# A Fourier-mixing and max-out feed-forward kernel: batch 0's loads in twelve transfers, and late work moved on GpSimd

## The chip, the cores and the metric

The kernel runs on one NeuronCore of a Trainium2 chip. The metric is the device time of one execution in microseconds (us); the time of a kernel is the median of its runs. Engines are named as in the profile: PE (TensorE, with PEld for its weight loads), DVE (VectorE), ACT (ScalarE), POOL (GpSimd) and SP (SyncE, which here only issues transfers).

## The reference

The input is x, 8 batches of 3072 rows by 256 columns, and four weight matrices. What is computed:

```
X = fft(fft(x, axis=1), axis=2).real          # 8 x 3072 x 256, then 24576 x 256
h = max(X @ w1, X @ w2, X @ w3)               # 24576 x 768
out = h @ w_out                               # 24576 x 256
```

## The kernel before

**Tiling.** The transform over the 3072 rows is split as 24 x 128. In a first stage ("s", lines 492 and 494; seven pieces per batch) PE multiplies batch b's rows with small 24-point matrices. The rows lie on 96 partitions (24 row groups times 4 column groups), once in natural order and once reversed. In a second stage ("k", lines 518 and 520; six pieces per batch) PE multiplies the result z with the table `tab`. This table has 13 row blocks of 384 values: sines, cosines, and negated sines. The transform over the 256 columns never runs on data: it is folded into the weights at the start (`prep_first`, `prep_second`), with the matrix `md`.

**Units.** The feed-forward part then runs per batch in 18 units (3 blocks of 512 tokens times 6 slices of the hidden width). A unit has four "plus" matmuls (538, 539), ACT's Relu (552), DVE's maximum (553), two "minus" matmuls (546), and about nine matmuls of the output layer (563). Of each 128 output rows (a slot, 12 in a batch), DVE makes `other` (590), POOL adds it to `even` (593), DVE adds that to PE's sum (613), and POOL and SP store the two halves (616, 626).

**Order.** The order on each engine is the order in which the program issues instructions. The dictionary `plan` (784 to 808) lists which extra work is issued at the end of which unit. `at(b, unit, fn)` adds to it. A unit number of 18 or more falls into the next batch. The engines run in order, so an instruction that waits holds all that stands behind it on its engine.

**Batch 0.** Its rows 112 to 127 come on the SP and ACT queues as fp32 (`xs_a`, 202). Rows 0 to 111 come on POOL's software queue, which casts them to bf16: three groups of 32 rows and one of 16, each group in four transfers (209 to 211). Then POOL issues w1 in two halves (219). SP issues raw w2 and w3 in four transfers (222); the first two wait for the second transfer of the last group of rows. SP has one queue, so batch 1's rows (409) stand behind these. ACT and DVE copy each group that has landed into a natural (`lay_rows`, 365) and a reversed (`turn_rows`, by way of `reverse`, 136) layout, each with the columns split between them. Among these copies DVE makes table angles (`tab_angles`, 270 and 274: two instructions for three row blocks), ACT the sines (`tab_sines`, 281 to 285), and DVE the argument `vm` of `md`. PE meanwhile runs 31 matmuls on table data (709) that nothing reads.

**POOL at the start.** After its transfers POOL waits for the last of DVE's copies (411), does some small constants and `rows_m` (412 to 237), the second halves of the differences w2 - w1 and w3 - w1 (`differences`, 186), and issues w_out (418). Then come batch 1's casts, per chunk of 32 rows one natural (151) and one reversed (154). `tab_minus` (289) negates the sines of table rows 7 to 9 at unit 1 and of rows 10 to 12 at unit 3, between the casts. PE's k pieces 3 and 4 read these.

**Later batches.** Rows are fetched by SP in four chunks (`fetch`, 771) into a ring of four buffers and cast by POOL. For batch 2 the 16 casts (4 chunks in 4 parts) are issued two per unit in units 14 to 21, counted from batch 0's first unit. For batches 3 to 7 they are one per unit from unit 6 of the batch two before.

Of the kernel before, what the change touches and what calls it, by code (L numbers as in the profile page):

```python
# [33 lines left out]
def kernel(  # L34
# [50 lines left out]
    two_row = consts.tile([128, 128], BF16, tag="two_row")  # L85
    half_pi = consts.tile([128, 64], FP32, tag="half_pi")
    w_late = consts.tile([128, 6 * 128], FP32, tag="w_late")
    twice = consts.tile([128, 256], FP32, tag="twice")
    sgn = consts.tile([128, 1], FP32, tag="sgn")
    dif = consts.tile([128, 1], FP32, tag="dif")  # L90
# [110 lines left out]
    rows_a = xs_a[:, 0:17 * 64].rearrange("p (bb dl) -> p bb dl", dl=64)  # L201
# [4 lines left out]
    iota(pidx, [[0, 1]], cm=1)  # L206
    j128 = gen.tile([128, 128], FP32, tag="j128")
    iota(j128, [[1, 128]])
    for r0 in (0, 32, 64):
        load_rows(nc.gpsimd, x0v[:, r0:r0 + 32, :], 0, r0, r0 + 32)  # L210
    last_part = load_rows(nc.gpsimd, x0v[:, 96:112, :], 0, 96, 112)

    def load_w(eng, wdst, wsrc, jh):
        return eng.dma_start(  # L214
# [5 lines left out]
    for jh in range(2):  # L220
        for wsrc, wdst in zip((moe_w2, moe_w3), raw_w):
            ld = load_w(nc.sync, wdst, wsrc, jh)
            if jh == 0:
                tc.add_manual_dep(ld.ins, last_part[1].ins.name, AFTER, reason="x first")

    rows_f = gen.tile([128, 12 * B], FP32, tag="rows_f")
    late = gen.tile([128, 1], FP32, tag="late")
# [23 lines left out]
    pi13 = gen.tile([128, 13], FP32, tag="pi13")  # L251
# [3 lines left out]
    step = gen.tile([128, 128], FP32, tag="step")  # L255
# [8 lines left out]
    def rows_of(r0, r1):  # L264
        return (w_late if r0 >= 7 else w)[:, (r0 % 7) * 128:(r0 % 7 + r1 - r0) * 128]

    def tab_angles(r0, r1):
        wr = rows_of(r0, r1)
        n = r1 - r0
        nc.vector.tensor_tensor(  # L270
            out=wr.rearrange("p (r j) -> p r j", j=128),
            in0=pi13[:, r0:r1].unsqueeze(2).to_broadcast([128, n, 128]),
            in1=step.unsqueeze(1).to_broadcast([128, n, 128]), op=ALU.subtract)
        nc.vector.scalar_tensor_tensor(out=wr, in0=wr, scalar=0.5, in1=wr,
                                       op0=ALU.is_gt, op1=ALU.subtract)

    def tab_sines(r0, r1, parts=(0, 1, 2)):
        wf = rows_of(r0, r1)
# [79 lines left out]
    def turn_rows(copy, r0, n, d0, d1):  # L358
        reverse(copy, xr0, x0_first[:, r0 * 64:(r0 + n) * 64], r0, n, d0, d1)
# [13 lines left out]
    lay_rows(on_act, xs_a, 112, 16)  # L373
    reverse(on_dve, xr0, xs_a, 112, 17)
    on_dve(out=xr0[:, 32, 17:18], in_=xs_a[:, 0:1])
    turn_rows(on_act, 0, 31, 32, 65)
    tab_angles(7, 10)
    tab_angles(10, 13)
    vm = gen.tile([128, 256], FP32, tag="vm")
    qm = gen.tile([128, 256], FP32, tag="qm")  # L380
    nc.vector.tensor_scalar(out=vm[:, 0:128], in0=dvec, scalar1=pidx, scalar2=64.0,
                            op0=ALU.mult, op1=ALU.add)
    lay_rows(on_act, bf_rows(0, 32), 0, 32)
    tab_sines(7, 10, (0, 1))
    turn_rows(on_dve, 31, 32, 32, 65)
    lay_rows(on_dve, bf_rows(32, 32), 32, 32)
    nc.vector.tensor_scalar(out=vm[:, 128:256], in0=dvec, scalar1=pidx, scalar2=None,
                            op0=ALU.mult)
    nc.vector.tensor_scalar(out=vm[:, 128:129], in0=pidx, scalar1=128.0, scalar2=64.0,
# [1 line left out]
    nc.vector.tensor_scalar(out=qm, in0=vm, scalar1=256.0 * ROUND, scalar2=None, op0=ALU.add)  # L391
    nc.vector.scalar_tensor_tensor(out=vm, in0=qm, scalar=-256.0 * ROUND, in1=vm,
                                   op0=ALU.add, op1=ALU.subtract)

    nc.scalar.activation(out=md[0], in_=vm, func=AX.Sin, scale=float(-2.0 * math.pi / 256.0))
    for (copy, a, b, c, d) in ((on_act, 54, 65, 20, 33), (on_dve, 32, 54, 0, 20)):
        turn_rows(copy, 63, 32, a, b)
        lay_rows(copy, bf_rows(64, 32), 64, 32, c, d)
    for (copy, a, b, c, d) in ((on_act, 58, 64, 22, 33), (on_dve, 32, 58, 0, 22)):
        turn_rows(copy, 95, 17, a, b)  # L400
        if copy is on_act:
            turn_rows(copy, 95, 16, 64, 65)
        laid = lay_rows(copy, bf_rows(96, 16), 96, 16, c, d)
    nc.vector.tensor_scalar(out=sgn, in0=pidx, scalar1=0.0, scalar2=None, op0=ALU.is_equal)
    nc.vector.tensor_scalar(out=sgn, in0=sgn, scalar1=2.0, scalar2=-1.0,
                            op0=ALU.mult, op1=ALU.add)
# [1 line left out]
    for ch in range(4):  # L408
# [5 lines left out]
    nc.gpsimd.memset(gw[:, 512:513], 0.0)  # L414
    nc.gpsimd.memset(gw[0:1, 512:513], 1.0)
    store_rows()
    differences(nc.gpsimd, 1)
    nc.gpsimd.dma_start(out=wout_bf.rearrange("p (jc c) -> p jc c", jc=NJC),
                        in_=moe_w_out.rearrange("(jc p) c -> p jc c", jc=NJC))

    def wide(t, cs):
        return t.rearrange("p (fc j) -> p fc j", fc=2)[:, :, cs]
# [348 lines left out]
    def fetch(b, ch):  # L771
        raw[b, ch] = load_chunk(b, ch)
# [11 lines left out]
    for (u, fn) in ((0, prep_some), (0, prep_some), (0, lambda: tab_sines(7, 10, (2,))),  # L784
                    (1, prep_some), (1, prep_some), (1, prep_some),
                    (2, lambda: m.k(2)), (2, prep_some), (2, lambda: tab_sines(10, 13, (0,))),
                    (3, prep_some), (3, lambda: tab_sines(10, 13, (1, 2))),
                    (4, lambda: m.k(3)), (4, prep_some), (5, prep_some), (5, l2_first),
                    (6, lambda: m.k(4)), (7, lambda: m.k(5)), (7, m.end),
                    (0, lambda: turn_chunk(1, 0)), (1, lambda: tab_minus(7, 10, nc.gpsimd)),  # L790
                    (2, lambda: turn_chunk(1, 1)), (3, lambda: tab_minus(10, 13, nc.gpsimd)),
                    (5, lambda: turn_chunk(1, 2)),
                    (7, lambda: turn_last(0)), (8, lambda: turn_last(1)),
                    (8, lambda: lay_last(0)), (9, lambda: lay_last(1)), (20, signed)):
        at(0, u, fn)
    for ch in range(4):
        at(0, (6, 7, 9, 11)[ch], lambda ch=ch: fetch(2, ch))
    for b in range(B - 1):
        for i, whats in enumerate(ahead):
            for what in whats:  # L800
                at(b, begin[b] + i if b else first_ahead[i], lambda b=b, what=what: piece(b + 1, what))
        if b + 2 < B:
            for ch in range(4):
                for part in range(4):
                    at(b, 6 + 4 * ch + part if b else 14 + 2 * ch + part // 2,
                       lambda b=b, ch=ch, part=part: turn_chunk(b + 2, ch, part))
                if b + 3 < B:
# [80 lines left out]
```

## Time and profile before

| what | value |
|---|---|
| median of three runs | 416.93 us (414.61 to 417.04) |
| the profiled execution | 416.61 us |
| its span, first to last instruction | 414.8 us |
| PE busy | 394.1 us, 95% of the span |
| POOL busy | 318.2 us, 77% |
| DVE busy | 309.2 us, 75% |
| ACT busy | 266.9 us, 64% |
| PE clock granted | 1.00 |
| DMA packets | 131175, 52.70 MB |

The profile is that of one execution. Its lines give a start, a duration, the engine, the line of the kernel, the operation, the tiles (out<-in) and, in brackets, how long the engine stood idle before and what ended that. The view by stage gives busy times and instruction counts of each engine between two times. A matmul's end is modelled, so short overlaps on PE mean nothing. The chain that ended last is followed back from the last instruction, at each step to what released it.

### The profile page before, as it was taken

The page shows a single profiled execution, that of the slowest core. Times are in us where ns is not written, and L with a number is a line of the kernel's source. Part 1 is how long each engine was busy: PE and PEld are TensorE (multiplying, and loading weights), DVE is VectorE, ACT ScalarE, POOL GpSimd, SP SyncE. Part 2 cuts the span into 40 slices and gives each one's busy share as a digit, 9 for nine tenths or more (in the row PEclk, how much of TensorE's full clock was granted, in tenths as well). Part 3 has the DMA queues.
Part 4 walks back from the last instruction along what each step waited for, and adds up shares of the span by engine and source line. Part 5 has one row for each costly group of instructions (what it writes and reads, how often), then busy time and mean ns, then how long its engine had stood idle before and what let it go on. Part 6 is the DMA issues. An engine that isn't in the chain of part 4 may idle for free.

```text
span 414.8 us, 9054 instructions
## 1 busy us (share of the span) xinstructions
PE 394.1 (95%) x3018; PEld 268.4 (65%) x3072; DVE 309.2 (75%) x559; ACT 266.9 (64%) x491; POOL 318.2 (77%) x429
## 2 busy tenths in 40 slices
PE   0988899989999999999999999999999999999996
PEld 0455667756676677667666666666676677766665
DVE  8887676776777777787668767687678777778884
ACT  7877667656765666756775666666676666655550
POOL 9846977999998888888878788888878844545651
PEclk9999999999999999999999999999999999999999
DMA  9998896574317852398216843287412222111314
GB/s 113 141 217 161 173 224 164 154 192 108 123 67 186 195 140 74 96 216 168 97 64 162 205 107 110 88 206 171 133 52 76 66 66 76 66 65 46 110 64 141
DMA packets 131175, 52.70 MB, mean 127 GB/s; under 512 B 113073, under 2 KB 128184, under 8 KB 131128
## 3 DMA queue, kind: packets, MB, share of 16 engines
q1 hardware_dynamic: 106496, 37.50, 36.6%
q0 software_dynamic: 23696, 14.29, 15.5%
q8 instruction: 24, 0.39, 0.4%
q10 hardware_dynamic: 936, 0.33, 0.3%
q14 instruction: 23, 0.19, 0.2%
HBM read 29.02 MB, written 25.17 MB: 131 GB/s over the span
## 4 chain that ended last, share of the span: by engine, by line
PE 86%; SPq 5%; POOL 4%; DMA 2%; issue 1%; DVE 0%; POOLq 0%
PE po L563 29%; PE pse L538 15%; PE pse L546 14%; PE pse L539 12%; SPq L103 4%; POOL x L103 3%; PE po L587 3%; PE ps L518 2%; PE ps L494 2%; PE ps L520 2%; PE ps L492 2%; PE pl L576 2%; DMA xs<-in_x_dram 1%; DMA x<-in_x_dram 1%; SPq L214 1%
## 5 line engine op out<-in xcount | busy, mean ns | idle before, releaser
L552 ACT ACTIVATE stmp<-pse 128x512 bf16<-128x512 f32 x288 | 171.2, 600 | 45.1 <-PE pse L539 26.7
L553 DVE TENSOR_TENSOR hp<-pse,stmp 128x512 bf16<-128x512 f32 x144 | 99.5, 691 | 89.4 <-ACT stmp L552 59.1
L616 POOL DMA_INDIRECT out_dram<-ot,rows_m x92 | 102.5, 1114 | 53.8 <-DVE ot L613 40.8
L538 PE MATMUL pse<-t,gE 128*128 128x512 bf16 x288 | 109.3, 379 | 2.1
L553 DVE TENSOR_TENSOR hm<-pse,stmp 128x512 bf16<-128x512 f32 x144 | 99.1, 689 | 3.7 <-ACT stmp L552 3.5
L539 PE MATMUL pse<-t,gO 128*128 128x512 bf16 x249 | 94.3, 379 | 0.0
L563 PE MATMUL po<-wout_bf,hp 128*128 128x256 bf16 x576 | 85.9, 273 | 0.0
L563 PE MATMUL po<-wout_bf,hm 128*128 128x256 bf16 x570 | 85.3, 273 | 0.1
L593 POOL TENSOR_TENSOR even<-even,other 128x256 f32<-128x256 f32 x92 | 66.5, 723 | 22.7 <-DVE other L590 20.4
L546 PE MATMUL pse<-t,gD 128*128 128x512 bf16 x273 | 82.4, 379 | 0.7
L563 PEld LDWEIGHTS <-hp 128*128 128x128 bf16 x576 | 56.2, 98 | 18.0 <-issue 2.8
L563 PEld LDWEIGHTS <-hm 128*128 128x128 bf16 x576 | 56.3, 98 | 16.6
L613 DVE TENSOR_TENSOR ot<-po,even 128x512 f32<-128x512 f32 x92 | 62.7, 682 | 0.7 <-POOL even L593 0.7
L151 POOL CAST x<-xs 96x544 bf16<-96x544 f32 (+2 forms) x51 | 58.7, 1155 | 4.6 <-DMA xs<-in_x_dram 4.6
L154 POOL CAST x<-xs 96x544 bf16<-96x544 f32 (+5 forms) x57 | 60.5, 1070 | 0.0
L522 ACT CAST t<-ps 128x512 bf16<-128x512 f32 x48 | 27.9, 585 | 36.5 <-PE ps L520 35.3
L546 PEld LDWEIGHTS <-gD 128*128 128x128 bf16 x288 | 27.9, 98 | 32.2
L499 ACT CAST z_all<-ps 128x480 bf16<-128x480 f32 x46 | 25.4, 559 | 35.2 <-PE ps L494 34.2
L590 DVE SCALAR_TENSOR_TENSOR other<-twice,po 128x256 f32<-128x256 f32 x92 | 43.8, 476 | 0.1
L539 PEld LDWEIGHTS <-gO 128*128 128x128 bf16 x288 | 28.1, 98 | 20.0 <-issue 1.8
L538 PEld LDWEIGHTS <-gE 128*128 128x128 bf16 x288 | 28.1, 98 | 19.9 <-issue 0.7
L579 ACT COPY even<-pl 128x512 f32<-128x512 f32 x46 | 27.0, 587 | 9.6 <-PE pl L576 9.2
(168 smaller groups left out, 382.9 us busy)
## 6 DMA issues: line engine op xcount, KB each, us to landing
xs<-in_x_dram SPq DMA_DIRECT2D x84, 198.0 KB
out_dram<-ot SPq DMA_DIRECT2D x90, 128.0 KB
xs<-in_x_dram SPq DMA_DIRECT2D x28, 192.0 KB
raw_w<-in_moe_w_dram SPq DMA_DIRECT2D x4, 384.0 KB
out_dram<-ot,rows_m POOLq DMA_INDIRECT x92, 3.8
x<-in_x_dram POOLq DMA_DIRECT2D x12, 96.0 KB, 5.3
out_dram<-ot SPq DMA_DIRECT2D x17, 64.0 KB
xs<-in_x_dram SPq DMA_DIRECT2D x32, 5.8 KB
```

Source lines behind the costliest of these rows:

```text
L151: nc.gpsimd.tensor_copy(v[:, d0:d1, ch * 32:ch * 32 + 32], xs[:, 0:32 * 64].rearrange("p (bb dl) -> p dl bb", dl=64)[:, d0:d1, :])
L154: reverse(lambda out, in_: nc.gpsimd.tensor_copy(out, in_), v[:, 33:66, :], xs, ch * 32, 33 if ch == 3 else 32, 32 + d0, 32 + d1)
L538: nc.tensor.matmul(pse[:, 0:n], gE[i][:, js], te, start=True, stop=False)
L539: nc.tensor.matmul(pse[:, 0:n], gO[i][:, js], to, start=False, stop=True)
L546: nc.tensor.matmul(pse, gD[i][:, js], to, start=False, stop=True, skip_group_check=True)
L552: nc.scalar.activation(out=stmp[:, 0:n], in_=pses[0][:, 0:n], func=AX.Relu)
L553: nc.vector.tensor_tensor(out=dst, in0=src3, in1=stmp[:, 0:n], op=ALU.max)
L563: nc.tensor.matmul(po, hcols(jc), wout_bf[:, jc * 256:(jc + 1) * 256], start=False, stop=(jc == NJC - 1), skip_group_check=True)
L590: nc.vector.scalar_tensor_tensor(out=other, in0=twice, scalar=po[:, 256:257], in1=po[:, 0:256], op0=ALU.mult, op1=ALU.subtract)
L593: nc.gpsimd.tensor_tensor(out=line[:, 256:512], in0=line[:, 0:256], in1=other, op=ALU.add)
L613: nc.vector.tensor_tensor(out=ot, in0=po, in1=lin, op=ALU.add)
L616: stored(nc.gpsimd.indirect_dma_start(out, bass.IndirectOffsetOnAxis(ap=rows_m[0:128 - lo, b * 12 + slot: b * 12 + slot + 1], axis=0), ot[ ...
```

## The change

- Batch 0's rows 0 to 111 are loaded in three groups of 40, 40 and 32 rows, twelve software transfers instead of sixteen. The copies into the two layouts follow these groups, and their split between ACT and DVE is new: of the middle group ACT lays 21 of 33 columns and DVE 12, DVE reverses all of it; of the last group ACT takes 9 columns of the reversed and 12 of the natural part.
- w1 has twelve transfers ahead of it on POOL's queue instead of sixteen, and the first loads of raw w2 and w3 wait for the first transfer of the last group.
- The angles of table rows 10 to 12 are no longer made by DVE among the copies, but by POOL after it has issued w_out, in three instructions instead of two, with a buffer `w_high` between them.
- `tab_minus(7, 10)` on POOL stands ahead of the differences; `tab_minus(10, 13)` is issued in unit 2, ahead of the second chunk's casts of batch 1.
- Batch 2's casts are spread over units 11 to 21, and batch 3's fourth fetch is issued at unit 24 instead of 22. On SP it now stands behind two stores of 64 rows.
- PE's order is the same, and its instructions are too.

```diff
-    for r0 in (0, 32, 64):
-        load_rows(nc.gpsimd, x0v[:, r0:r0 + 32, :], 0, r0, r0 + 32)
-    last_part = load_rows(nc.gpsimd, x0v[:, 96:112, :], 0, 96, 112)
+    for (r0, r1) in ((0, 40), (40, 80), (80, 112)):
+        last_part = load_rows(nc.gpsimd, x0v[:, r0:r1, :], 0, r0, r1)
...
-                tc.add_manual_dep(ld.ins, last_part[1].ins.name, AFTER, reason="x first")
+                tc.add_manual_dep(ld.ins, last_part[0].ins.name, AFTER, reason="x first")
...
-    def tab_angles(r0, r1):
+    def tab_angles(r0, r1, eng=nc.vector):
         wr = rows_of(r0, r1)
         n = r1 - r0
-        nc.vector.tensor_tensor(
+        eng.tensor_tensor(
             out=wr.rearrange("p (r j) -> p r j", j=128),
             in0=pi13[:, r0:r1].unsqueeze(2).to_broadcast([128, n, 128]),
             in1=step.unsqueeze(1).to_broadcast([128, n, 128]), op=ALU.subtract)
...
+        else:
+            eng.tensor_scalar(out=w_high[:, 0:n * 128], in0=wr, scalar1=0.5, scalar2=None,
+                              op0=ALU.is_gt)
+            eng.tensor_tensor(out=wr, in0=w_high[:, 0:n * 128], in1=wr, op=ALU.subtract)
...
-    turn_rows(on_act, 0, 31, 32, 65)
+    turn_rows(on_act, 0, 39, 32, 65)
+    lay_rows(on_dve, bf_rows(0, 40), 0, 40)
     tab_angles(7, 10)
-    tab_angles(10, 13)
...
-    lay_rows(on_act, bf_rows(0, 32), 0, 32)
     tab_sines(7, 10, (0, 1))
-    turn_rows(on_dve, 31, 32, 32, 65)
-    lay_rows(on_dve, bf_rows(32, 32), 32, 32)
+    turn_rows(on_dve, 39, 40, 32, 65)
...
+    lay_rows(on_act, bf_rows(40, 40), 40, 40, 12, 33)
+    lay_rows(on_dve, bf_rows(40, 40), 40, 40, 0, 12)
     nc.scalar.activation(out=md[0], in_=vm, func=AX.Sin, scale=float(-2.0 * math.pi / 256.0))
-    for (copy, a, b, c, d) in ((on_act, 54, 65, 20, 33), (on_dve, 32, 54, 0, 20)):
-        turn_rows(copy, 63, 32, a, b)
-        lay_rows(copy, bf_rows(64, 32), 64, 32, c, d)
-    for (copy, a, b, c, d) in ((on_act, 58, 64, 22, 33), (on_dve, 32, 58, 0, 22)):
-        turn_rows(copy, 95, 17, a, b)
+    for (copy, a, b, c, d) in ((on_act, 55, 64, 21, 33), (on_dve, 32, 55, 0, 21)):
+        turn_rows(copy, 79, 33, a, b)
         if copy is on_act:
-            turn_rows(copy, 95, 16, 64, 65)
-        laid = lay_rows(copy, bf_rows(96, 16), 96, 16, c, d)
+            turn_rows(copy, 79, 32, 64, 65)
+        laid = lay_rows(copy, bf_rows(80, 32), 80, 32, c, d)
...
     store_rows()
+    tab_minus(7, 10, nc.gpsimd)
     differences(nc.gpsimd, 1)
     nc.gpsimd.dma_start(out=wout_bf.rearrange("p (jc c) -> p jc c", jc=NJC),
                         in_=moe_w_out.rearrange("(jc p) c -> p jc c", jc=NJC))
+    tab_angles(10, 13, nc.gpsimd)
...
-                    (0, lambda: turn_chunk(1, 0)), (1, lambda: tab_minus(7, 10, nc.gpsimd)),
-                    (2, lambda: turn_chunk(1, 1)), (3, lambda: tab_minus(10, 13, nc.gpsimd)),
+                    (0, lambda: turn_chunk(1, 0)), (2, lambda: tab_minus(10, 13, nc.gpsimd)),
+                    (2, lambda: turn_chunk(1, 1)),
...
-                    at(b, 6 + 4 * ch + part if b else 14 + 2 * ch + part // 2,
+                    at(b, 6 + 4 * ch + part if b else 11 + 11 * (4 * ch + part) // 16,
                        lambda b=b, ch=ch, part=part: turn_chunk(b + 2, ch, part))
                 if b + 3 < B:
-                    at(b, UNITS + (0, 1, 2, 4)[ch], lambda b=b, ch=ch: fetch(b + 3, ch))
+                    at(b, UNITS + (0, 1, 2, 4 if b else 6)[ch], lambda b=b, ch=ch: fetch(b + 3, ch))
```

`pi13`, `step` and `w_high` become constants that live on, since POOL now reads them later.

More of the change, by code (lines that the diff above doesn't have):

```diff
@@ L87 @@
     w_late = consts.tile([128, 6 * 128], FP32, tag="w_late")
+    pi_all = consts.tile([128, 64], FP32, tag="pi_all")
+    pi13 = pi_all[:, 0:13]
+    step = consts.tile([128, 128], FP32, tag="step")
+    w_high = consts.tile([128, 3 * 128], FP32, tag="w_high")
     twice = consts.tile([128, 256], FP32, tag="twice")
@@ L200 @@
     xs_a = xs_pool.tile([96, 33 * 64], FP32, name="xs", tag="xs")
-    rows_a = xs_a[:, 0:17 * 64].rearrange("p (bb dl) -> p bb dl", dl=64)
+    rows_a = xs_a.rearrange("p (bb dl) -> p bb dl", dl=64)
     load_rows((nc.sync, nc.sync, nc.scalar, nc.scalar), rows_a[:, 0:16, :], 0, 112, 128)
@@ L250 @@
     nc.vector.tensor_scalar(out=p128, in0=pidx, scalar1=1.0 / 128.0, scalar2=None, op0=ALU.mult)
-    pi13 = gen.tile([128, 13], FP32, tag="pi13")
     nc.vector.tensor_scalar(out=pi13, in0=j128[:, 0:13], scalar1=pidx, scalar2=1.0 / 3072.0,
                             op0=ALU.mult, op1=ALU.mult)
-    step = gen.tile([128, 128], FP32, tag="step")
     near = gen.tile([128, 128], FP32, tag="near")
@@ L273, in tab_angles @@
             in1=step.unsqueeze(1).to_broadcast([128, n, 128]), op=ALU.subtract)
-        nc.vector.scalar_tensor_tensor(out=wr, in0=wr, scalar=0.5, in1=wr,
-                                       op0=ALU.is_gt, op1=ALU.subtract)
+        if eng is nc.vector:
+            eng.scalar_tensor_tensor(out=wr, in0=wr, scalar=0.5, in1=wr,
+                                     op0=ALU.is_gt, op1=ALU.subtract)
+        else:
+            eng.tensor_scalar(out=w_high[:, 0:n * 128], in0=wr, scalar1=0.5, scalar2=None,
+                              op0=ALU.is_gt)
+            eng.tensor_tensor(out=wr, in0=w_high[:, 0:n * 128], in1=wr, op=ALU.subtract)
     def tab_sines(r0, r1, parts=(0, 1, 2)):
```

## The prediction

> **What bounds the kernel now.** I read the page's busy slices, then the chain that ended last, then PE's timeline at the places where that chain leaves PE, then POOL's timeline and the waits. The chain by engine says how much is PE's alone:
>
> ```profile
> PE 86%; SPq 5%; POOL 4%; DMA 2%; issue 1%; DVE 0%; POOLq 0%
> ```
>
> The other 14% (58 us) lie in the first 46 us and in one place near 90. By stage (us, busy and count of PE, PEld, DVE, ACT, POOL, then clock, DMA, GB/s):
>
> ```profile
> 18.00:24.00 6.00, 4.81 (x81) 4.23 (x82) 4.57 (x13) 3.83 (x10) 1.77 (x10) 1.00 1.10 300
> 36.00:45.00 9.00, 7.47 (x49) 4.66 (x49) 4.62 (x9) 4.37 (x9) 6.30 (x5) 1.00 0.74 159
> 56.00:86.00 30.00, 29.79 (x253) 21.28 (x255) 20.88 (x36) 20.35 (x40) 24.73 (x33) 1.00 0.71 182
> 86.00:94.00 8.00, 6.99 (x55) 4.65 (x54) 5.95 (x10) 4.09 (x8) 7.67 (x11) 1.00 0.66 163
> 140.00:400.00 260.00, 258.07 (x1983) 176.95 (x2018) 196.64 (x335) 167.49 (x307) 197.20 (x269) 1.00 0.40 111
> ```
>
> From 94 on PE is full (258.07 of 260) and the clock is 1.00, so nothing this change does there pays; it can only bring that stretch forward. What stands before it is PE's idle time, in brackets:
>
> ```profile
> 22.09 0.34 PE L432 MATMUL psg<-d_bf,md_all 128*128 128x384 bf16 x1 [0.64 <-DVE d_bf L186]
> 25.95 0.32 PE L432 MATMUL psg<-d_bf,md_all 128*128 128x384 bf16 x1 [0.37 <-POOL d_bf L186]
> 35.67 0.27 PE L518 MATMUL ps<-tab,z_all 128*128 128x256 bf16 x1 [0.77 <-POOL tab L289]
> 43.87 0.27 PE L518 MATMUL ps<-tab,z_all 128*128 128x256 bf16 x1 [1.31 <-POOL tab L289]
> 91.74 0.27 PE L587 MATMUL po<-gw,t 128*128 128x257 bf16 x1 [0.94 <-DVE ot L613]
> ```
>
> Before them PE starts at 18.55, when the last copies of batch 0 end. Matmul ends are modelled, so I count a stall from when the next matmul could have begun: 0.80, 0.54, 0.93, 1.47, 1.11, and 0.24 more at 93.11. POOL's timeline shows why the tables are late: they stand behind casts that wait for batch 1's rows.
>
> ```profile
> 24.26 1.64 POOL L186 TENSOR_TENSOR d_bf<-raw_w,w_bf 128x768 bf16<-128x768 f32 x1 [3.59 <-DMA raw_w<-in_moe_w_dram]
> 26.37 1.65 POOL L186 TENSOR_TENSOR d_bf<-raw_w,w_bf 128x768 bf16<-128x768 f32 x1 [0.47 <-DMA raw_w<-in_moe_w_dram]
> 34.43 1.19 POOL L289 TENSOR_SCALAR tab<-tab 128x384 bf16<-128x384 bf16 x1
> 38.70 2.00 POOL L151 CAST x<-xs 96x1056 bf16<-96x1056 f32 x1 [3.09 <-DMA xs<-in_x_dram]
> 42.64 1.17 POOL L289 TENSOR_SCALAR tab<-tab 128x384 bf16<-128x384 bf16 x1
> 63.26 0.98 POOL L616 DMA_INDIRECT out_dram<-ot,rows_m  x1 [2.80 <-DVE ot L613]
> ```
>
> **The change part by part.** The profiled execution took 416.61 (span 414.8, 1.8 around it), 0.32 under the median 416.93. I sum against 416.61 and follow PE's lead over before.
>
> *Twelve transfers.* POOL's sixteen issues take 0.71 to 1.26, median 0.85, whatever their rows; the last begins at 14.58 and lands about 17.4 (DVE is released at 17.50). Each from the ninth on waits for the one eight before it, which has landed by then (the first at 6.8, the ninth issued at 8.18), so the queue's semaphores hold nothing up, w1's two issues included. Twelve end near 1.47+0.2+12x0.85 to 12x1.06 (by rows) = 11.9 to 14.4. The engines then bound: the DMA view counts 12156 software packets from 4.5 to 14.5, but only 1826 from 14.5 to 17, which at the first rate need 1.5 of the 2.5 us. So rows 80-112 land near 16.2 (16.0, plus a little for the weights that now share). Behind them DVE copies 759+672 elements, 1.40 by its rows (704 in 0.69), and ACT 297+32+384, 1.6 by its rows (352 in 0.71). Fewer, longer copies (ACT two instructions less, DVE one) save their fixed part, under 0.1 each. Earlier work does not delay the last ones: DVE copies rows 0-40 at 10.0 (1.27), makes the table rows 7-10 (1.04) and vm's first half, waits at 12.5 for rows 40-80 (near 13.2), and has vm done near 15.8; so it loses two table instructions (1.1) but waits 0.7. ACT reads the same rows, takes its md sine behind vm and ends it near 16.2, as the third group lands. PE starts at 16.2+1.65+0.2 = 18.05: **lead 0.5**. Ends: 0.8 (the warm matmuls end at 17.76) and -1.9 (each issue 1.26, landing 2.0 after the last, at 18.6).
>
> *Weights sooner.* SP's raw_w loads wait for the ninth of twelve transfers, not the fourteenth of sixteen: 11/14 of the rows, near 14.0 instead of 16.04. The engines, however, only gain the 1.0 to 1.4 that x ends earlier. So w1 (issued near 13 instead of 15.37, but behind x on the same queue), raw_w, and SP's next in line, batch 1's rows, come 1.3 earlier; ends 0 and 2.0 (issue times alone). DVE's first difference waits no more (w1's half at 19.5, DVE free at 20.0), and the lead grows by 0.5 to **1.0**. POOL begins its small instructions when DVE's last copy ends, 17.9 instead of 18.40, and is through with them (2.2) and with the table below (1.18) at 21.3; the weights' second halves are there near 22.6, with 0.33 from landing to start as before. So POOL's differences still wait for data: they end 1.3 earlier, so the stall at 25.95 shrinks and by 28 the lead is **1.3**.
>
> *Late tables.* tab_minus(7,10), 1.18, now runs in POOL's 3.59 of waiting, so the stall at 35.67 (0.93) goes. tab_angles(10,13) becomes three POOL instructions behind the w_out issue: from L593 (256 two-input, 0.72), L186 (768, 1.64) and L289 (384 one-input, 1.18) they are 0.95+1.18+0.95 = 3.1, from 27.6 to 30.7. ACT's sine of them stands at 31.63-1.3 = 30.3 with the next units' stmp behind it: 0.4 of new wait. Next late is w_out: PE's weight load at L461 already waited 0.2 for it near 36.2; it is issued and lands 1.3 earlier, near 34.9, where PE, with ACT's wait, would come at 34.3. So of 0.93 nothing is left by L461 and the lead stays **1.3**. The first chunk of batch 1 lands near 29.0, so POOL casts it from 30.7 to 34.7 and no later work waits for that. tab_minus(10,13) moves ahead of the second chunk's casts, into the 3.09 idle; PE's 1.47 at 43.87 goes: **2.75** at 45.
>
> *POOL after 43.* Its chain gains the 1.1 of the moved table and the 1.3 of the earlier rows, 2.4 in all. Before, batch 1's casts ended at 55.87 and PE began that batch's matmuls at 56.22; PE can thus lead by at most 2.4+0.25 = **2.65** here.
>
> *Batch 2's casts.* 16 casts (near 1.09 each) over units 11 to 21 instead of 14 to 21 fill POOL's idle 2.80 and 1.44. Before, POOL was the later one at 91 by 1.1+0.24; with up to 4.2 of work moved forward that stall goes: lead **4.0**. fetch(3,3) goes two units later, past two stores on SP; its rows are first cast at unit 36 (near 120) and SP's store no longer stands behind its wait. Cost 0. Cover: 25 us between load and use.
>
> Sum: 416.61 - 0.5 - 0.5 - 0.3 - 1.45 + 0.1 - 1.35 = **412.6**.
>
> **Rivals.** (A) *The data comes sooner still:* loads shift by 2.0 and nothing holds PE to the bound at 56: 2.0+1.36+1.35 = 4.7, and 0.7 of the small ACT and DVE waits between 24 and 41 goes: 411.2. For it: SP stood 11.5 us at that wait. Against: the engines were busy.
>
> (B) *POOL's late table holds ACT.* If the broadcast operands double its price to 6.2, ACT waits 3.4 instead of 0.4; the 0.93 at 35.67 and later slack cover half, and the lead at 45 falls to 0.45: 416.61-0.45-1.35 = 414.8. Against: L593 and L186 agree on a slope of 1.8 ns.
>
> (C) *Batch 2's stall stays.* Casts ahead of L593 at units 11 to 13 make DVE's L613 wait early, or POOL only keeps pace: per unit 1.45 casts (1.6) and 0.67 slots (1.2) are 2.8, PE's unit is 2.7. Then 1.35 isn't won: 414.0. For it: POOL at 7.67 of 8.00 from 86 to 94. Against: the 4.2 idle before.
>
> (D) *Slower: the early weights take the engines from group three.* raw_w's packets would begin near 15.1 (1.1 after issue, as before), with 0.9 us of x left, about 68 packets an engine. From 18 to 24, 1503 large packets took some 70 ns each on an engine; one for one, raw_w's 64 per engine delay x by 4.5: PE starts at 22.3, every later stall is absorbed, and 415.4 is left. At the 4.6 to 1 that the trace shows in the us from 31 (299 packets of w_out's queue, 65 of SP's), turned round, the rows of batch 1 pass x as well, another 4.9: 420.2. It becomes slower than before once rows 80-112 land after 21.8. The Trainium skill's "DMA: Bandwidth & Descriptors", Queues, rings and completion order, says that each engine goes round the queues packet by packet, a packet holding several descriptors; by it something like the one-for-one case, 415.4, would come. That share is open in this trace. Against (D): where the two queues met at 31, it was SP's that starved, and SP's issues stood 2.9 to 4.0 while w1 moved.
>
> **How the numbers follow.** Forecast 0.50 (its own range 411.6 to 413.7), A 0.08, B 0.16, C 0.12, D 0.14 (0.08 near 415.4, 0.06 at 417 to 421). Leaving out half of A and D's upper part, the range is 411.2 to 415.5. About 1%, 4.17 of 416.93, is what a measurement here can tell from no change: faster means under 412.76. That is 0.6 of the forecast and A with a bit of C: 0.40; slower (over 421.1) 0.04; same 0.56.
>
> **What would show it.** PE's first L492 near 18.05; psg's stall at 22.09 under 0.15; SP's first raw_w issue near 14.0; no PE wait on POOL's table; POOL's three table instructions near 3.1 and ACT's wait ahead of the sine under 0.6; w_out as PE's new wait near 35; batch 1's first matmul near 53.6, just behind POOL's last cast; no L613 wait near 88. It is wrong if the third group lands after 17.4 (D), if ACT stands over 1 at the sine (B), or if L587 or L494 still waits near 88 (C).

## The result and the profile after

The changed kernel takes 413.64 us (median of 9 runs, 412.57 to 413.96) and the kernel before 416.89 on the same chip (9 runs, 414.61 to 417.21): a ratio of 0.9927, 95% interval 0.991 to 0.9943, or 3.25 us less. That is within the 1% that the forecast called no change. In a second measurement, side by side on one chip, the changed kernel came to 413.5 and the kernel before to 415.74: 0.9944 (0.9926 to 0.9962), 2.24 us less. The changed kernel agrees in both; the kernel before differs by 1.15. The profiled execution of the changed kernel took 412.57 (span 410.8), its fastest run, so the two profiled executions stand 4.04 apart: the forecast's sum of 4.0 is met there, and missed by 1.04 at the median. One execution of e6_old_casts below took 1081.53 us and is left out of its median.

Most line numbers of the kernel have moved by 4 (L492 is now L496, L587 is L591). The chain by engine:

```profile
PE 92%; POOL 3%; DVE 2%; issue 1%; DMA 1%; ACT 0%; DVEq 0%; ACTq 0%; POOLq 0%
```

PE's share went from 86% to 92%, and SP's queue is gone from it. The same stages as before:

```profile
18.00:24.00 6.00, 5.23 (x83) 4.26 (x82) 5.17 (x13) 4.42 (x12) 4.56 (x12) 1.00 1.05 308
36.00:45.00 9.00, 8.78 (x60) 5.62 (x60) 6.24 (x11) 6.21 (x13) 7.97 (x5) 1.00 0.90 171
56.00:86.00 30.00, 29.79 (x246) 21.09 (x249) 20.69 (x36) 21.16 (x41) 28.98 (x38) 1.00 0.73 189
86.00:94.00 8.00, 7.82 (x68) 5.45 (x68) 6.02 (x11) 5.22 (x10) 7.39 (x10) 1.00 0.74 165
140.00:400.00 260.00, 258.00 (x1967) 176.61 (x2003) 196.77 (x335) 167.43 (x306) 195.04 (x269) 1.00 0.40 109
```

PE gained 0.42 of 6, 1.31 of 9 and 0.83 of 8 in the three stages with stalls; from 140 on nothing changed. POOL, with batch 2's casts spread out, is now full from 56 to 86 (28.98 of 30, before 24.73). PE's timeline at the places that stalled before:

```profile
19.01 0.20 PE L496 MATMUL ps<-m24f,nat 96*128 96x96 bf16 x1 [0.74 <-DVE sgn L406]
21.84 0.34 PE L436 MATMUL psg<-d_bf,md_all 128*128 128x384 bf16 x1
34.38 0.27 PE L522 MATMUL ps<-tab,z_all 128*128 128x256 bf16 x1
88.02 0.27 PE L591 MATMUL po<-gw,t 128*128 128x257 bf16 x1
```

Only the first line still has a wait behind it in brackets. It is the start, and it is later than before (18.55), not sooner. POOL's timeline:

```profile
21.99 1.19 POOL L295 TENSOR_SCALAR tab<-tab 128x384 bf16<-128x384 bf16 x1
23.16 3.26 POOL L190 TENSOR_TENSOR d_bf<-raw_w,w_bf 128x768 bf16<-128x768 f32 x2
27.31 0.85 POOL L271 TENSOR_TENSOR w_late<-pi_all,step 128x384 f32<-128x384 f32 x1
28.26 1.18 POOL L279 TENSOR_SCALAR w_high<-w_late 128x384 f32<-128x384 f32 x1
29.52 1.00 POOL L281 TENSOR_TENSOR w_late<-w_high,w_late 128x384 f32<-128x384 f32 x1
37.03 2.00 POOL L155 CAST x<-xs 96x1056 bf16<-96x1056 f32 x1 [1.41 <-DMA xs<-in_x_dram]
51.82 1.21 POOL L177 CAST x<-xs 96x495 bf16<-96x495 f32 x2
```

The differences (L190) now follow each other with no wait (before 3.59 and 0.47), the three table instructions stand behind them, and the last cast of batch 1 ends at 53.03 instead of 55.87.

**Where the 4 us came from.** PE's order is the same in all kernels, so its lead can be read off: the time of a group of matmuls in the first trace of before minus its time in another trace.

| PE's lead over before, us | forecast | changed kernel | what lies between |
|---|---|---|---|
| first matmul of batch 0 (before 18.55) | 0.5 | -0.46 | twelve transfers |
| third psg to the next k pieces (before 28 to 31) | 1.3 | 0.57 | weights sooner |
| behind both table stalls (before 44.08) | 2.75, capped at 2.65 | 2.91 | late tables |
| behind batch 2's stall (before 95) | 4.0 | 3.97 | batch 2's casts |

Term by term that is -0.46 instead of +0.5, +1.03 instead of +0.8, +2.34 instead of +1.35 and +1.06 instead of +1.35. The sum is right because two errors of one microsecond cancel. From 95 to the end the lead goes from 3.97 to 4.04, so the later fetch of batch 3 cost nothing there.

The forecast counted two of the stalls of before 0.21 too large each. In that trace the second of a unit's two minus matmuls has no record ahead of 35.67 and ahead of 91.74. The first line is from before, the second is the same place in e1 (below), where both have one:

```profile
34.52 0.38 PE L546 MATMUL pse<-t,gD 128*128 128x512 bf16 x1
34.85 0.59 PE L546 MATMUL pse<-t,gD 128*128 128x512 bf16 x2
```

So these stalls were 0.72 and 0.90, not 0.93 and 1.11. The leads compare the same matmuls and are not touched by this.

### The profile page after: what moved, and what is told of

Its sections match the earlier page's. It is cut to its first block, busy times and chain, and to the rows that moved or that the text cites. A ratio compares the mean times of both kernels' runs of the same rounds, so it can differ in the third digit from the quotient of the medians.

```text
span 410.8 us, 9043 instructions
## 1 busy us (share of the span) xinstructions
PE 393.8 (96%) x3018; PEld 268.9 (65%) x3072; DVE 308.8 (75%) x556; ACT 266.6 (65%) x489; POOL 319.8 (78%) x428
## 3 DMA queue, kind: packets, MB, share of 16 engines
q0 software_dynamic: 23632, 14.29, 15.7%
## 4 chain that ended last, share of the span: by engine, by line
PE 92%; POOL 3%; DVE 2%; issue 1%; DMA 1%; ACT 0%; DVEq 0%; ACTq 0%; POOLq 0%
PE po L567 31%; PE pse L542 16%; PE pse L550 15%; PE pse L543 13%; PE po L591 3%; PE ps L496 3%; PE ps L522 3%; POOL x L107 3%; PE ps L498 3%; PE ps L524 3%; PE pl L580 2%; DMA x<-in_x_dram 1%; PE psg L436 1%; DVE hm L557 1%; PE psw L465 0%
```

## The experiments

Three groups of four kernels, each group beside the kernel before on the same chip (its medians there: 415.43, 415.74 and 415.27). The lead is that of the profiled execution, against the first trace of before as above, behind the psg group (at 31), behind the tables (at 44), and at the end of the span.

| kernel | median us | ratio to before (95%) | first matmul | lead 31 | lead 44 | lead at end |
|---|---|---|---|---|---|---|
| e1_casts_alone | 414.85 | 0.9988 (0.9974 to 1.0002) | 18.58 | -0.32 | 0.38 | 1.48 |
| e2_tables_alone | 414.62 | 0.9985 (0.9967 to 1.0003) | 19.03 | 0.08 | 2.42 | 2.36 |
| e3_loads_alone | 414.85 | 0.9989 (0.9973 to 1.0004) | 19.03 | 0.55 | 2.28 | 2.51 |
| e4_raw_after_last | 413.30 | 0.9955 (0.9939 to 0.997) | 19.78 | -0.20 | 2.14 | 3.30 |
| after_again | 413.50 | 0.9944 (0.9926 to 0.9962) | 19.30 | -1.10 | 1.23 | 2.37 |
| e5_tables_and_casts | 413.56 | 0.9949 (0.9927 to 0.997) | 19.09 | -0.50 | 1.35 | 2.58 |
| e6_old_casts | 414.06 | 0.9964 (0.9945 to 0.9983) | 18.70 | 0.89 | 3.23 | 3.37 |
| e7_md_first | 412.78 | 0.9925 (0.9898 to 0.9952) | 19.23 | 0.35 | 2.69 | 3.54 |
| e8_raw_after_group_two | 419.34 | 1.0097 (1.0078 to 1.0116) | 23.81 | -6.22 | -3.88 | -2.79 |
| e9_last_group_24 | 412.94 | 0.995 (0.9931 to 0.9968) | 19.00 | -0.44 | 1.90 | 2.95 |
| e10_two_us_more_on_POOL | 413.55 | 0.9965 (0.9946 to 0.9983) | 18.39 | 0.25 | 2.09 | 1.70 |
| e11_rows_96_on_hardware | 419.89 | 1.0119 (1.0097 to 1.0141) | 24.67 | -6.80 | -4.46 | -3.38 |

**The casts alone.** The kernel before with

```diff
-                    at(b, 6 + 4 * ch + part if b else 14 + 2 * ch + part // 2,
+                    at(b, 6 + 4 * ch + part if b else 11 + 11 * (4 * ch + part) // 16,
```

and the later fetch. 

> The kernel before with batch 2's casts in units 11 to 21 (and fetch(3,3) two units later), nothing else. Waits theory: POOL uses its idle 2.80 and 1.44 near 60 to 66, PE's stalls at 91.74 and 93.11 (1.1 and 0.24) go, all before stays: span 413.4 to 413.8, about 1.2 less, ratio 0.997. Rival (POOL only keeps pace, so PE waits for L613 or the casts elsewhere between 56 and 93): ratio 1.000, with new gaps of PE before 90.

The stall near 91 is gone from its trace; the lead goes from 0.39 ahead of it to 1.45 behind it, 1.06. That is near the 1.2 expected. The medians give 0.58, and the interval of their ratio takes in no change (1.0).

**The tables alone.** The kernel before with `tab_angles(10, 13, nc.gpsimd)` behind w_out's issue and the two `tab_minus` in their new places. 

> The kernel before with only the table work on POOL in the new places (tab_minus(7,10) ahead of the differences, tab_angles(10,13) on POOL behind w_out, tab_minus(10,13) ahead of the second chunk). Waits theory: PE's stalls on POOL's table at 35.67 and 43.87 go; w_out's landing near 36.2 holds PE there, POOL's chain to batch 1's casts gets 1.1 shorter, so PE leads by 1.3 at 56; the stall near 91 stays: about 1.3 less in all, ratio 0.997, with a PE wait of 0.5 to 0.9 on w_out at L461's place. Rival (the three POOL instructions hold ACT's sine and the units behind it): ACT waits over 1 us ahead of the sine, ratio 0.999 to 1.003.

No matmul waits for a table, and the lead grows by 2.34 between 31 and 44. Batch 2's stall is still there, at 89.55 with 0.90: the lead of the tables alone does not outgrow it, nor is any of it lost there. The new wait for w_out that was expected did not come, and ACT did not wait for POOL's table. The medians give 0.81 where 1.3 was expected, and the interval takes in no change.

**The loads alone.** The changed kernel with tables and casts put back. 

> The changed kernel with tables and casts put back: only the twelve transfers, the new split of the copies and the earlier weights are left (DVE again makes the late angles, 1.1 us, in its wait for rows 40 to 80). Waits theory: PE starts no sooner than before (18.5 to 19.2), the stalls at 22.09 and 25.95 go, batch 1's rows come 1.5 us earlier and with them both POOL tables, so the waits on the tables stay near 0.8 and 1.3 but come 1.5 earlier; the stall near 91 stays: about 1.5 less, ratio 0.9965. Rival (the start decides: what PE loses at its first matmul it keeps): ratio 0.999 to 1.001.

The old table places now cost PE less. Of the two waits for a table one is left above the timeline's limit:

```profile
34.74 0.27 PE L521 MATMUL ps<-tab,z_all 128*128 128x256 bf16 x1 [0.17 <-POOL tab L295]
```

The two are 0.33 and 0.28, where before they were 0.72 and 1.47; the expectation had them stay near 0.8 and 1.3. So loads and tables work on the same stalls. When the weights come sooner, so do batch 1's rows behind them on SP's queue, and POOL's casts, which wait for these rows ahead of each table, begin at 29.40 and 36.44 instead of 30.34 and 38.70. POOL's timeline of e3:

```profile
29.40 2.02 POOL L155 CAST x<-xs 96x1056 bf16<-96x1056 f32 x1 [1.71 <-DMA xs<-in_x_dram]
36.44 2.00 POOL L155 CAST x<-xs 96x1056 bf16<-96x1056 f32 x1 [1.76 <-DMA xs<-in_x_dram]
```

**Raw weights behind all rows.** The changed kernel, with the raw weights waiting for the last of the twelve transfers:

```diff
-                tc.add_manual_dep(ld.ins, last_part[0].ins.name, AFTER, reason="x first")
+                tc.add_manual_dep(ld.ins, last_part[3].ins.name, AFTER, reason="x first")
```

> The changed kernel with raw w2 and w3 held until the last of the twelve transfers has landed (about 16.6) instead of the ninth (14.6). Waits theory: SP's packets begin near 17.9 instead of 17.0, DVE's and POOL's differences still have their data in time, but batch 1's second chunk, for which POOL waits, comes 0.9 later: POOL's chain and PE behind it lose 0.6 to 0.9 by 56, ratio to the changed kernel 1.002, PE's first matmul unchanged at 19.0. Rival (early weights take the engines from the last group of rows): the last group lands earlier, PE's first matmul comes 0.3 or more sooner, and the time is the same or less than the changed kernel's.

SP issues them at 17.44 instead of 14.60. The first matmul is not sooner for it (19.78), so nothing shows that the raw weights took time from the rows in the changed kernel; there SP's first packet, at 16.99, came behind the rows' last, at 16.30. The lead at 31 and at 44 is 0.77 lower than the changed kernel's first, which is the later start: the later weights themselves cost nothing more, where 0.6 to 0.9 was expected; the ratio is not to be told from the changed kernel's.

**The changed kernel again.** 

> The changed kernel once more, beside the kernel before on the chip of the other runs of this call. If its gain is one of PE's waits, it is the same on every chip: ratio 0.991 to 0.994, and PE's waits as in its first profile (0.10 us ahead of the first psg, none on a table, about 0.3 us near 88). The rival, that the first chip's kernel before ran long (416.9 against 415.4 on the chip of the single parts, whose gains sum to only 2.0 us), gives a ratio near 0.9952 (2.0 us of 415.4).

The ratio, 0.9944, is nearer to the rival's 0.9952, though 0.9927 lies just inside its interval. The trace shows a wait that the first one had not. First PE's waits from 18.5 to 56 (us in total, times, longest), then POOL's timeline:

```profile
PE psg L436 <- POOL d_bf L190: 1.2, 1, 1.2
PE ps L496 <- ACT nat L371: 0.6, 1, 0.6
```

```profile
25.36 3.24 POOL L190 TENSOR_TENSOR d_bf<-raw_w,w_bf 128x768 bf16<-128x768 f32 x2 [1.89 <-DMA raw_w<-in_moe_w_dram]
```

The second halves of the weights, there by 23.16 in the first trace, when POOL began, landed near 25.3 here, and w1's second half at 23.78 instead of 20.11. The issues were the same (raw weights at 14.56 and 14.60, w1 at 14.24 and 14.01). Only when they land differs, by over 2 us from one execution to the next, and PE's lead at 31 is 1.7 lower.

**All but the loads.** The kernel before with the new tables and casts. 

> The kernel before with the new places of the table work and with batch 2's casts in units 11 to 21; its loads, its copies and its weights are the old ones. If the parts add (0.81 us for the tables alone, 0.58 us for the casts alone), it comes out 1.4 us under the kernel before, ratio 0.9966. If the parts need one another (the casts can only give back what the tables have made of a lead), it shows more than that: the stalls of before at 35.67, 43.87 and near 91 sum to 3.7 us, ratio 0.991. First matmul 18.5 to 19.0, stall at the first psg 0.4 to 0.8 us, none on a table, none near 90.

413.56 is 2.18 us under the kernel before: more than the 1.4 of parts that add, less than the 3.7 of parts that need one another, and the interval (to 0.997) takes in the first alone. Beside it stands 413.50 for the whole change on the same chip: 0.06 us is what the loads, copies and weights add to the other two parts, with an interval of the difference of about 1.2 us each way (the ratios' half widths are 0.0018 and 0.0021).

**All but the casts.** The changed kernel with the old units for batch 2. 

> The changed kernel with batch 2's casts back in units 14 to 21 and the fetch back at unit 22. If the step on the casts holds, PE's stall on the maximum's sum near 88 to 91 comes back with 0.9 to 1.3 us, and the time is 0.9 to 1.3 us above the changed kernel of this call (ratio to before 0.0022 to 0.0031 higher). If POOL, which is 2.8 us earlier out of batch 1's casts, has room for them there by itself, the stall stays under 0.3 us and the times are equal within 0.4 us.

The stall is back:

```profile
88.46 0.27 PE L591 MATMUL po<-gw,t 128*128 128x257 bf16 x1 [0.67 <-DVE ot L617]
```

With what follows at 89.82 it is 0.84 + 0.23 = 1.07, although POOL was out of batch 1's casts at 52.24, 0.8 earlier than in the changed kernel. The medians differ by 0.56, less than the half width of either interval (about 0.8). In the traces the step on the casts is right; the medians do not show it by themselves.

**DVE's order at the start.** The changed kernel with the four instructions for md's argument ahead of the middle group's reversed copy:

```diff
-    turn_rows(on_dve, 39, 40, 32, 65)
     nc.vector.tensor_scalar(out=vm[:, 128:256], in0=dvec, scalar1=pidx, scalar2=None,
...
+    turn_rows(on_dve, 39, 40, 32, 65)
```

> The changed kernel with DVE's last four instructions for md's argument ahead of the reversed copy of rows 40 to 79, where DVE waited 1.02 us for those rows. If DVE's own queue sets the last copies, as the trace of the changed kernel shows (no wait between 14.41 and 18.85), the first matmul comes 0.5 to 1.0 us earlier, near 18.0 to 18.5; if the transfers set it, it stays near 19.0. At the end PE can keep of that only what POOL's batch 1 casts leave, which hold its lead near 48 to 53: at most 0.3 us by that theory, 0.5 to 1.0 us by the rival that the whole start is PE's.

What made me try it is DVE's timeline in the changed kernel: a wait for the second group, and then work without a gap until the last copy ends.

```profile
14.41 1.39 DVE L140 COPY back<-x 96x1320 bf16<-96x1320 bf16 x1 [1.02 <-DMA x<-in_x_dram]
16.54 0.42 DVE L396 SCALAR_TENSOR_TENSOR vm<-qm,vm 128x256 f32<-128x256 f32 x1
16.88 0.59 DVE L371 COPY nat<-x 96x480 bf16<-96x480 bf16 x1
17.39 0.81 DVE L140 COPY back<-x 96x759 bf16<-96x759 bf16 x1
18.13 0.72 DVE L371 COPY nat<-x 96x672 bf16<-96x672 bf16 x1
```

In e7 the four instructions fill that wait, and DVE then waits for the third group:

```profile
15.74 0.58 DVE L371 COPY nat<-x 96x480 bf16<-96x480 bf16 x1
17.60 0.83 DVE L140 COPY back<-x 96x759 bf16<-96x759 bf16 x1 [1.28 <-DMA x<-in_x_dram]
18.35 0.74 DVE L371 COPY nat<-x 96x672 bf16<-96x672 bf16 x1
```

The first matmul stays at 19.23: the rows, landed at 17.48, set it, and 1.5 us of copies behind them. But these rows came 0.86 later than in the changed kernel's first trace (16.62), where DVE was busy until 17.39. So DVE's own queue does not set the start alone, and what the new order gives when the rows come at 16.62 this trace does not show. The time is the lowest of all, but its interval overlaps the changed kernel's, so it is not shown to be faster.

**Raw weights earlier.** The changed kernel with the raw weights waiting for the first transfer of the second group of rows. 

> The changed kernel with the first loads of raw w2 and w3 waiting for the first transfer of the second group of rows (landing near 12) instead of the third's (near 14.5), so that SP issues them near 12. If a packet of SP's hardware queue takes turns with the software queue's on the DMA engines (the slower rival of the forecast), its 1536-byte packets show between 13 and 16, the last rows land later than 17.5 and the first matmul comes after 19.5; the time is 0.5 to 1.5 us above the changed kernel (413.5 beside 415.7 in the call before). If SP's packets wait until the software queue's rows are through, as they did in both first traces (first packet 16.99 behind a last one at 16.33; 17.26 behind 17.11), none shows before 16, the first matmul stays at 18.7 to 19.3 and the time is equal within 0.4 us.

Slower than the kernel before by 4.07 us, and my theory fell: packets of SP's queue do not wait for the software queue's rows. SP issued at 11.78 and its packets began at 12.9. The DMA view by queue (packets, MB, share of 16 engines) of e8 from 14 to 16, when the changed kernel had 1577 software packets and none of SP's:

```profile
q1 hardware_dynamic: 282, 0.41, 75.1%
q0 software_dynamic: 774, 0.07, 68.4%
```

and of e8 from 16 to 18:

```profile
q1 hardware_dynamic: 380, 0.56, 89.6%
q0 software_dynamic: 430, 0.04, 36.1%
```

From 16 on the two queues move about one packet each in turn, but one of SP's has 1536 bytes and one of the rows 128. The last rows land at 22.07 instead of 16.62, and PE comes to a standstill:

```profile
23.81 0.24 PE L498 MATMUL ps<-m24f,nat 96*128 96x96 bf16 x1 [4.95 <-ACT nat L373]
```

The Trainium skill, "DMA: Bandwidth & Descriptors", Queues, rings and completion order, says that an engine goes round the queues that have work, packet by packet; this trace agrees from 16 to 18 (380 and 430 packets), and less well from 14 to 16 (282 and 774). The idle stretch has a second price, in the stages of e8 (clock is the third value from the end):

```profile
20.00:24.00 4.00, 0.19 (x3) 0.22 (x4) 1.74 (x5) 1.58 (x3) 0.23 (x2) 0.67 1.22 181
24.00:30.00 6.00, 5.90 (x75) 5.38 (x73) 4.49 (x8) 2.99 (x7) 5.53 (x11) 0.65 0.88 185
30.00:36.00 6.00, 5.79 (x34) 3.24 (x34) 5.17 (x10) 5.13 (x11) 5.80 (x6) 1.00 0.83 141
```

The granted clock was 0.65 from 24 to 30, and 5.26 of late start became 6.74 by the next pieces; the stalls that were there to absorb it then gave back 2.9 by 44.

**A smaller last group.** e7 with groups of 44, 44 and 24 rows. 

> The kernel of e7_md_first with groups of 44, 44 and 24 rows instead of 40, 40 and 32. If the start is the landing of the last group plus the copies of that group (1.57 us for 32 rows on DVE in e7: 0.83 and 0.74), the first matmul comes 0.4 us sooner against the landing (copies of 1.2 us), near 18.8, and the time is 0.4 us under e7's, ratio to before near 0.9915. If a smaller last group only moves DVE's queue ahead of it (44 rows of the second group take 1.46 us there instead of 1.33), the first matmul stays near 19.2 and the time is e7's within 0.2 us.

The copies of the last group did end sooner, at 18.65 (ACT's; 19.16 in e7), but the rows had also landed sooner, at 16.73 instead of 17.48. Behind the landing they took 1.92 instead of 1.68: DVE, without a wait from 15.34 on, was at the second group until 17.26, as the second case of the expectation had it. And PE's first matmul was at 19.00, without a wait: the 31 matmuls whose results nothing reads were still running. PE's timeline in the changed kernel:

```profile
9.59 8.68 PE L713 MATMUL warm<-tab 128*128 128x512 bf16 x31 [9.59 <-ACT m0r L350]
```

and in e9:

```profile
9.79 9.38 PE L713 MATMUL warm<-tab 128*128 128x512 bf16 x31 [9.79 <-ACT m0r L350]
```

They run 0.43 us apart at first and 0.22 later, and the change-over came at 13.4 in the one and at 14.9 in the other. psg then stalled as well, by 0.43 and 0.77. The raw weights were issued later (15.59), but DVE did not wait for them: its two differences took 1.28 and 1.84, where they took 0.95 and 1.04 in the changed kernel. POOL worked beside them, and began first each time. DVE's and POOL's timelines of e9:

```profile
20.83 1.28 DVE L190 TENSOR_TENSOR d_bf<-raw_w,w_bf 128x768 bf16<-128x768 f32 x1
22.60 1.84 DVE L190 TENSOR_TENSOR d_bf<-raw_w,w_bf 128x768 bf16<-128x768 f32 x1
```

```profile
20.79 1.19 POOL L295 TENSOR_SCALAR tab<-tab 128x384 bf16<-128x384 bf16 x1
21.98 1.65 POOL L190 TENSOR_TENSOR d_bf<-raw_w,w_bf 128x768 bf16<-128x768 f32 x1
```

**More work on POOL.** The changed kernel with two more instructions ahead of batch 1's third chunk:

```diff
-                    (5, lambda: turn_chunk(1, 2)),
+                    (5, more_pool), (5, lambda: turn_chunk(1, 2)),
```

> The changed kernel with two more instructions of 128x384 on POOL (1.9 us by the rows of 0.85 and 1.00) ahead of the casts of batch 1's third chunk; they write a buffer that nothing reads. If POOL's casts of batch 1 hold PE's lead, as the forecast has it with its cap of 2.65 us, their end moves from 53.0 to 54.9 and PE's first matmul of batch 1 (53.3 in the first trace of the changed kernel) waits 0.9 to 1.6 us for them; the time rises by as much, ratio to the kernel before near 0.9975. If there is slack that the forecast did not see, no wait on POOL's casts shows near 53 and the time rises by less than 0.4 us.

They take 2.08 in all. PE's lead falls from 2.09 to 0.69 in one place, a wait for a sum that POOL made behind a cast. PE's and POOL's timelines of e10:

```profile
49.89 0.27 PE L596 MATMUL po<-gw,t 128*128 128x257 bf16 x1 [1.31 <-DVE ot L622]
```

```profile
42.41 2.08 POOL L171 TENSOR_TENSOR w_high<-w_late 128x384 f32<-128x384 f32 x2
44.43 2.04 POOL L155 CAST x<-xs 96x1056 bf16<-96x1056 f32 x1
46.43 2.00 POOL L158 CAST x<-xs 96x1056 bf16<-96x1056 f32 x1
48.40 0.72 POOL L602 TENSOR_TENSOR even<-even,other 128x256 f32<-128x256 f32 x1
```

So POOL does hold PE when it is 2 us later, and the 1.40 lost is within what was expected; it bites at the outputs between the casts (L602, then DVE's L622), not first at batch 1's matmuls. At the median it shows less: the ratio is 0.0021 (0.9 us) above that of after_again, inside the intervals.

**More rows on the hardware queues.** e7 with rows 96 to 127 as fp32 on SP and ACT, laid and reversed by POOL, and groups of 40, 40 and 16:

```diff
-    lay_rows(on_act, xs_a, 112, 16)
-    reverse(on_dve, xr0, xs_a, 112, 17)
-    on_dve(out=xr0[:, 32, 17:18], in_=xs_a[:, 0:1])
+    on_dve(out=xr0[:, 32, 33:34], in_=xs_a[:, 0:1])
+    reverse(nc.gpsimd.tensor_copy, xr0, xs_a, 96, 33)
+    lay_rows(nc.gpsimd.tensor_copy, xs_a, 96, 32)
```

> The kernel of e7_md_first with rows 96 to 127 (instead of 112 to 127) as fp32 on the SP and ACT queues, so that the software queue has 96 rows left in groups of 40, 40 and 16; POOL, idle there, lays and reverses the 32 rows. The first two traces show about 1000 packets a microsecond on the software queue from 4 to 13 us, and POOL's issue of 960 of them takes 0.87 us: the one or the other sets the pace of the rows. If POOL's issue sets it, 1536 packets fewer end the rows' transfers 1.4 us sooner, the first matmul comes near 17.5 to 18.0 and the time is 1.0 to 1.5 us under e7's, ratio near 0.989. If the DMA engines are full, the rows on the hardware queue take as much from them as they leave, the last rows land near 16.5 as before, the first matmul comes at 18.4 to 19.0 and the time is within 0.4 us of e7's. POOL's two casts of 2.0 us each could also slow DVE's copies beside them, which would show as longer instructions there.

Slower than the kernel before by 4.62, mainly for a reason that the question did not ask. DVE's and POOL's timelines of e11:

```profile
15.97 4.87 DVE L387 TENSOR_SCALAR vm<-dvec,pidx 128x128 f32<-128x128 f32 x1
```

```profile
16.66 2.21 POOL L140 CAST back<-xs 96x1056 bf16<-96x1056 f32 x2
18.77 1.97 POOL L371 CAST nat<-xs 96x1056 bf16<-96x1056 f32 x1
```

An instruction of DVE that takes 0.28 in the changed kernel (at 13.11) took 4.87 and ended at 20.84, just as POOL's three casts were through (20.74); ACT waited 3.31 for it. That POOL's casts held it is read from this one trace, and not all of it fits: the record of the DVE instruction begins 0.69 ahead of the first cast. It is also not the clean trial it was to be: the rows' first packets on the software queue came at 5.3 instead of 3.8, POOL's last four issues each waited for earlier rows to land, and DVE had its first rows at 13.69 instead of 10.81. Whether POOL's issue or the engines set the pace of the rows stays open.

## Why the prediction came out as it did

**Twelve transfers: wrong, by 0.96.** The forecast's 18.05 came out as 19.01. The issues ended at 13.3, inside the bounds given (11.9 to 14.4), and the last rows landed at 16.62 (forecast 16.2). The failed part is what lies between: rows 40 to 79 were taken to land near 13.2 and md's argument to be done near 15.8, and they landed at 14.29 and it was done at 16.96, so DVE began the last copies 0.8 behind the rows' landing and ended them at 18.85. Over all kernels with the new loads the first matmul is at 18.39 to 19.78 (e8 and e11 apart), with the old ones at 18.55 to 19.09: the twelve transfers moved the start by nothing that shows. e7 and e9 suggest why no single cure works: three things end within a microsecond of one another, the last landing plus its copies, DVE's own work, and the 31 matmuls. The forecast had the third as its upper end (17.76) but no spread for it.

**Weights sooner: right in the profiled execution (1.03 for 0.8), not as a step to count on.** The wait at psg is 0.10 (forecast under 0.15), SP's issue is at 14.60 (near 14.0), and POOL's differences did not wait at all, where the forecast still had them wait. POOL came to them at 23.16 instead of 21.3: it began 1.0 later, and its cast to `rows_m` took 1.04 instead of 0.26. But in after_again they waited, for 1.89, and they did in e3 and e10. Between the kernels with the new loads the lead at 31 ranges from -1.10 to 0.89 (without e8 and e11), with the old ones from -0.50 to 0.08. The landing of transfers that share the engines is a spread of 2 us, and the forecast put one number there.

**Late tables: too small, 2.34 for 1.35.** Both stalls went, as forecast (0.72 and 1.47), and with them 0.15 that PE had waited for w_out behind the first; the two new waits that were to eat the first did not come. POOL's three instructions took 0.85, 1.18 and 1.00, against 0.95, 1.18 and 0.95. ACT's sine began at 31.06, after POOL's end at 30.52, because PE and ACT were 0.7 later than forecast; and w_out landed at 32.63 rather than 34.9. Where POOL was later against PE, the wait of rival B did show, in small: in e5 and e10 ACT waited 0.46 and 0.47 for POOL's table, and PE 0.41 for ACT.

**POOL's cap: right in kind, not reached. The casts: right.** PE led by 2.91 at 56, over the cap of 2.65, since POOL's last cast ended 2.84 earlier rather than 2.4. Batch 1's first matmul came at 53.31, 0.28 behind that cast and without a wait (forecast: near 53.6, just behind it); e10 shows that 2 us more of POOL's work there costs PE 1.40. The casts were worth 1.06 of lead in e1 and in the changed kernel, and 1.07 came back in e6; the forecast's 1.35 counted the matmul without a record (0.21) as stall, and 0.08 of the stall stays at 88.02.

**The slower rival (D): its mechanism is real, its condition was not met.** The forecast had SP's packets begin 1.1 after their issue, near 15.1, amid the last rows. In the changed kernel they began 2.4 after it, at 17.0, behind the rows' last packet at 16.3; why it took so long stays open. e8 met the condition: 282 of SP's packets between 14 and 16, the last rows at 22.07 (the forecast's point from which it decides was 21.8), and 419.34, between the 415.4 and the 420.2 that the forecast gave. Its one-for-one case is what the packets show from 16 on; that the rest of the price is the clock and the earlier meeting is argued, not tried.

**The size.** Added up in one pair of executions the forecast is 0.03 off; against the medians it says 4.3 where 2.24 and 3.25 were measured. The single parts' gains, 0.58, 0.81 and 0.58, sum to 1.97. What the forecast lacked was the spread of the kernel before's own stalls: it took the two table stalls as fixed (0.72 and 1.47 once counted with the missing record), and e1, which does not touch them, shows 0.74 and 0.90 in its profile. That the medians' shortfall is this spread was not tried by itself.

## What to carry to other kernels

Follow one lead along the engine that is full, and give each term a spread from how much its transfer's landing varies: a wait that hangs on two queues sharing the DMA engines differed by 2 us between executions of one kernel. A load that is safe behind another may be so by a margin of a microsecond only: here the issue 2.8 us sooner turned a gain into 4 us of loss. And parts that relieve the same stall must not be added, so undo each from the whole as well as trying each alone.

## What the runs showed of the hardware

- PE idle for 5 us lost its clock: granted 0.65 for the six microseconds from 24 in e8 and 0.64 in e11 (idle 4.95 and 5.72), 1.00 in the changed kernel.
- Beside POOL's casts, one after another for 4.1 us, a DVE instruction of 0.28 took 4.87 (e11). The Trainium skill, "SBUF — State Buffer", SBUF: two separate sides, has GpSimd and those DVE instructions that run in a 2-port mode or read two SBUF inputs hold a shared pair of ports for a whole instruction, whoever starts first, the other being blocked. The trace agrees in the length: DVE's instruction ended only behind the last of three of POOL's. It does not show why DVE, recorded from 15.97, lost to a cast from 16.66.
- Which of the two lost time elsewhere went with which began first. In six traces (the changed kernel's two, e3, e4, e6, e7) DVE's first difference began 0.03 or 0.04 ahead of POOL's cast to `rows_m`, and the cast took 1.04 instead of 0.26. In e9 POOL's table began 0.04 ahead of DVE's difference, which took 1.28 instead of 0.95, and POOL's difference 0.62 ahead of DVE's second, which took 1.84 instead of 1.04.
- From a raw-weight transfer's issue on SP to its first packet it took 1.1 to 1.2 us in seven traces and 1.9 to 2.5 in seven (2.4 in the changed kernel: 14.60 to 16.99). Rows still under way do not separate them: in e5 (16.18 to 17.26) and e8 (11.78 to 12.94) it was 1.1 to 1.2 with rows still moving. What does stays open.
